# Group 2 of a fused attention and MLP kernel: 16 pairs of W2 rows in seven products behind the output projection, and the softmax maximum in two passes

## The chip, the core and the metric

The kernel runs on one core of one Trainium2 chip. The metric is the device time of one execution in microseconds, as the median of several runs. TensorE does the matmuls and VectorE, ScalarE and GpSimd the rest; SyncE issues most DMAs, and GpSimd those that add into SBUF. In the trace they are PE (PEld: its weight loads), DVE, ACT, POOL and SP.

## The reference

```python
def reference(A_x, A_wqkv, A_wo, B_x, B_w1, B_b1, B_w2, B_b2):
    # B, S, D, F = 1, 2048, 576, 4608; H = 32 heads of 18; window W = 8, dilation 2
    x = A_x
    h = x + _A_ref(_layernorm(x), A_wqkv, A_wo)         # windowed attention
    return h + _B_ref(_layernorm(h), B_w1, B_b1, B_w2, B_b2)

    # _A_ref: qkv = x @ wqkv; each position looks at itself and at the seven
    #         positions 2, 4, ..., 14 before it; softmax over the 8; o @ wo
    # _B_ref: gelu(layernorm(x) @ w1 + b1) @ w2 + b2
```

## The kernel before

The 2048 rows are 16 tiles of 128 rows; row p of tile j is position 16 p + j, so a window of dilation 2 lies in tiles of the same parity. Even tiles keep K and V in `kv_ring[0]` and odd tiles in `kv_ring[1]`; a *halo* load replaces a tile's K or V by the rows shifted by one partition once its last user is done. The tiles are treated in `GROUPS` of two: (14, 12), (10, 8), (6, 4), (2, 0), (15, 13), (11, 9), (7, 5), (3, 1), numbered 0 to 7 by `k`. All instructions stand in the order in which the program issues them on each engine (a manual schedule); nothing reorders them.

One round of the loop over `k` runs these stages for group `k` on TensorE, with the attention of later groups beside them on VectorE:

- **MLP1** (`pm`, line 228): 324 matmuls of 64 rows each; ScalarE's GELU writes `h_all` (line 586). Lists `m1[0]` to `m1[3]` hold what other engines issue ahead of its four visits.
- **Output projection** (`pw`, line 228) for the two tiles c and d of group k + 1: 36 matmuls of 64 rows, from `oT`. `oT` is the attention output turned by DMA: `send_o` stores it to DRAM (`td`, lines 210 and 211) and `read_o` reads it back transposed (line 447).
- **MLP2** (`po`, line 693) for group k: W2's 36 row blocks are 18 pairs. `ROWS[k]` pairs go through seven products (a Strassen-like scheme for 2 x 2 blocks: two tiles by two row blocks, two column halves) and the others through eight plain matmuls (`plain`, steps "11", "12", "21", "22"). All are matmuls of 128 rows. Groups 0 and 1 use plain matmuls throughout (line 605).

The seven products need sums of W2 blocks (`w2_sums`, line 663), made once and kept, and sums of `h_all` blocks (`h_sums`, line 673), made per group. Both are VectorE instructions. `t_slot` and `s_slot` say where the sums lie: in dead parts of `kv_ring`, `x_all` and `q_all`. With pairs beyond `SR` = 12, three H sums of four pairs lie in `q_all` 15, 13 and 11 until `kv_ring[1]` is free.

In `mlp2_fast` the list `steps` is the order on TensorE; a step name calls what `hooks` (the dictionary `x`) holds. "wo" is the output projection; "hc" and "h" are the residual sums with LN2 (`ln2_h`, line 475; `ln2_act`, whose root is the GpSimd power at line 500) and H sums; (n, rows) is product n; "b", "d" and "f" are ScalarE copies of one bank into another (line 782); "6", "7", "in", "exp" and "4" hold LN2's stores and transposing reads (`hnT`, line 516), attention and reloads; "o1" is the output sum of the second tile (line 724).

Attention for the tiles e and f of group k + 2 is, on VectorE: the QK product (`att_qk_a`, line 352) with its additions (361, 370), the softmax maximum and its subtraction (`att_max`, lines 376 and 377), after ScalarE's exponential the sum and division (`att_den`, lines 403 to 405), and in the next round the two PV products (line 409) with additions. `att_qk_a` behind an LN2 is made to wait for the root (`root`).

Before the change, group 2 differs from groups 3 to 6:

```python
ROWS = {2: 12, 3: 16, 4: 16, 5: 16, 6: NM, 7: NM}
steps = [(1, all_), "b", "wo", "hc", "h", "e", (2, all_), ...]          # group 2
steps = ["wo", "hc", (1, all_), "b", "h", "e", (7, lo), (2, all_), ...] # groups 3 to 5
x["7"] += [c_(att_qk_one, f, 1) if k > 2 else c_(att_qk_b, f, 1), c_(att_max, (e, f))]
```

In group 2 the QK product of tile f stands ahead of the H sums (in `m1[3]`), and only its additions stand in "7".

Of the kernel before, what the change touches and what calls it, by code (L numbers as in the profile page):

```python
# [13 lines left out]
F16 = mybir.dt.float16  # L14
# [3 lines left out]
def kernel(  # L18
# [13 lines left out]
    P = 128  # L32
# [23 lines left out]
    GROUPS = [ATT_ORDER[i:i + 2] for i in range(0, NT, 2)]  # L56
# [14 lines left out]
    x_all = wpool.tile([P, NT, D], BF16, name="x_all")  # L71
    q_all = wpool.tile([P, NT, D], BF16, name="q_all")
# [492 lines left out]
    NM = FT // 2  # L565
# [73 lines left out]

    SR = 12  # L640
    ring1_free = [False]
    RING_T = 3 * SR * P

    def s_slot(t, m0, m1):
        if t == 2:
            return h_block(0, 1, m0, m1)
        i = (0, 1, None, 2)[t]
        if m0 < SR:
            return ring_blocks(0, (i * SR + m0) * P, m1 - m0, P)
        if not ring1_free[0]:  # L650
            return q_all[:, 15 - 2 * i, (m0 - SR) * P:(m1 - SR) * P].bitcast(F16).rearrange("p (m c) -> p m c", c=P)
        return ring_blocks(1, 6 * HALF + (i * (NM - SR) + m0 - SR) * P, m1 - m0, P)

    def h_block(odd, i, m0, m1):
# [50 lines left out]
    def c_(fn, *a):  # L705
        return lambda: fn(*a)
# [1 line left out]
    def halves(ap):  # L708
        return ap.rearrange("p (g c) -> p g c", g=2)

    def mlp2_fast(g, rows, tags, wo, hooks, first_wo=False):
        last, summed = wo is None, rows < NM
        q, p, r, s = tags
        j0, j1 = g
        af = psum_pair(q, "po")
        a, f = (af[:, n, 0:HALF] for n in range(2))
        b, d = psum_pair(p, "po")[:, 0, 0:HALF], None
        o0, o1 = (new_o(j, summed) for j in g)
        flat = kv_ring[1][:].rearrange("p w t d -> p (w t d)")
        rest = halves(flat[:, W * 2 * D - 2 * D:W * 2 * D].bitcast(F32))  # L720
        bank = {1: a, 2: a, 3: f, 4: b, 6: b}

        def add(out, x, y):
            nc.vector.tensor_tensor(out=out, in0=x, in1=y, op=ALU.add)

        def last_out():
            nc.vector.tensor_copy(out=o0[:, HALF:HALF + HALF // 2], in_=f[:, 0:HALF // 2])
            nc.scalar.copy(out=o0[:, HALF + HALF // 2:D], in_=f[:, HALF // 2:HALF])
            nc.sync.dma_start(out=out3[:, j0, HALF:D], in_=o0[:, HALF:D])

        def out0(n0, n1):
            if summed:
                nc.scalar.copy(out=halves(o0), in_=af[:, :, 0:HALF])
                return
            add(halves(o0)[:, n0:n1], af[:, n0:n1, 0:HALF], halves(x_of(j0))[:, n0:n1])
            nc.sync.dma_start(out=out3[:, j0, n0 * HALF:n1 * HALF], in_=o0[:, n0 * HALF:n1 * HALF])

        def out1():
            if summed:
                add(o1[:, HALF:D], bank[5], o1[:, 0:HALF])  # L740
                add(o1[:, 0:HALF], b, o1[:, 0:HALF])
                out_sum(j1)
                return
            add(o1[:, 0:HALF], b, rest[:, 0])
            add(o1[:, HALF:D], bank[5], rest[:, 1])
            nc.sync.dma_start(out=out3[:, j1, :], in_=o1)

        def do_rest():
            if summed:
                nc.scalar.copy(out=o1[:, 0:HALF], in_=bank[7])  # L750
                return
            add(rest, bank[7].unsqueeze(1).to_broadcast([P, 2, HALF]), halves(x_of(j1)))

        def take():
            bank[7], bank[5] = (psum_pair(tag, "po")[:, 0, 0:HALF] for tag in (r, s))

        lo, hi, all_ = (0, SR), (SR, rows), (0, rows)
        seed = {"b": (1, 6), "d": (6, 5), "f": (5, 3)}
        does = {
            "wo": lambda: wo((r, s)), "e": take, "rest": do_rest, "o1": out1,  # L760
            "o0": lambda: last_out() if last else out0(0, 2), "lo": lambda: out0(0, 1),
            "11": lambda: plain(0, 0, a, rows), "12": lambda: plain(0, 1, f, rows),
            "21": lambda: plain(1, 0, b, rows), "22": lambda: plain(1, 1, bank[5], rows),
        }
        if rows < NM:
            steps = [(1, all_), "b", "wo", "hc", "h", "e", (2, all_), "11", (6, all_), "d", "6", "7", (7, all_), "rest"] if not first_wo \
                else ["wo", "hc", (1, all_), "b", "h", "e", (7, lo), (2, all_), (6, all_), "6", "d", "rest", "7", "11"] if rows == SR \
                else ["wo", "hc", (1, all_), "b", "h", "e", (7, lo), (2, all_), (6, all_), "6", "7", "d", "11", (7, hi), "rest"]
            steps += ["in", (5, all_), "f", "exp", (4, all_), "21", "22", "o1", "4", (3, all_), "12", "o0", "3"]
        elif not last:  # L770
            steps = ["wo", "hc", (1, all_), "b", "h", "e", (7, lo), (6, all_), "6", "d", "7", (2, all_), (7, hi), "rest", "in",
                     (5, all_), "f", (4, all_), "o1", "4", (3, all_), "o0"]
        else:
            steps = ["e", (1, lo), (7, lo), (1, hi), "b", "h", (7, hi), "rest", (6, all_), "d", (2, all_), "lo",
                     (5, all_), "f", (4, all_), "o1", (3, all_), "o0"]
        for step in steps:
            if isinstance(step, tuple):
                product(step[0], bank[step[0]], *step[1])
            elif step == "f" and last:
                add(f, bank[5], x_of(j0)[:, HALF:D])  # L780
            elif step in seed:
                nc.scalar.copy(out=bank[seed[step][1]], in_=bank[seed[step][0]])
            else:
                call([does[step]] if step in does else hooks.get(step, ()))
# [22 lines left out]
    with tc.manual_schedule(engines={ENG.PE, ENG.Activation, ENG.DVE, ENG.SP, ENG.Pool}):  # L807
# [223 lines left out]
        def wo_visit(*duos, fill=False):  # L1031
            visit([wo_duo(j, tag) for j, tag in duos], (lambda: [ahead[0]() for _ in range(2)]) if fill else None)

        ROWS = {2: 12, 3: 16, 4: 16, 5: 16, 6: NM, 7: NM}
        p, q, r, s = "ABDC"

        gelu_table()
        for k, g in enumerate(GROUPS):
            c, d = GROUPS[k + 1] if k + 1 < len(GROUPS) else (None, None)
            e, f = GROUPS[k + 2] if k + 2 < len(GROUPS) else (None, None)  # L1040
            m1, mid, ia, ib, late_wo = {0: []}, {}, {}, {}, None
# [28 lines left out]
            if k < 2:  # L1070
# [1 line left out]
                mlp2_tile(g, 0, "D", ia)  # L1072
                mlp2_tile(g, 1, "C", ib)
                continue
            rows = ROWS[k]
            x = {n: [] for n in ("hc", "h", "6", "7", "in", "exp", "4", "3")}
            if 2 < k < 7:
                m1[0] += [c_(pv_sum, c), c_(send_o, c), c_(pv_sum, d), c_(read_o, c), c_(send_o, d), c_(read_o, d)]
            if k < 6:
                m1[1] = m1.get(1, []) + [c_(att_qk_one, e, 0)]  # L1080
                m1.setdefault(3, [])
                if k == 2:
                    m1[0] += [c_(pv_sum, d), c_(send_o, d), c_(read_o, d)]
                    m1[3] += [c_(w2_sums, 0, 8, (2, 3)), c_(w2_sums, 8, 12, (2, 3)), c_(w2_sums, 12, 14, (0, 1)), c_(w2_sums, 14, 16, (0, 1)),
                              c_(att_qk_a, f), c_(halo, f, 1)]
                early = {2: (), 5: (0,)}.get(k, (0, 2))
                if k == 3:
                    m1[3] += [c_(w2_sums, 12, 14, (2, 3)), c_(w2_sums, 14, 16, (2, 3))]
                m1[3] += [c_(h_sums, 0, min(rows, SR), early)]
                if k == 5:  # L1090
                    x["h"] += [c_(h_sums, 0, SR, (2,)), c_(h_sums, 0, SR, (1, 3))]
                else:
                    x["h"] += [c_(h_sums, 0, SR, [t for t in range(4) if t not in early])]
                if rows > SR:
                    x["h"] += [c_(h_sums, SR, rows)]
                x["7"] += [c_(att_qk_one, f, 1) if k > 2 else c_(att_qk_b, f, 1), c_(att_max, (e, f))]
                x["exp"] += [c_(exps, e, f)]
                x["4"] += [c_(att_den, e, f)]
            else:
                if k == 6:  # L1100
                    ring1_free[0] = True
                    m1[1].append(c_(w2_sums, 16, NM))
                m1[3] = m1.get(3, []) + [c_(h_sums, 0, SR)]
                if k == 7:
                    mid[3] = {1: [c_(h_sums, SR, 16)]}
                    x["h"] += [c_(h_sums, 16, NM)]
            if k + 3 < len(GROUPS):
                x["in"] += [c_(reload_x, GROUPS[k + 3])]
            wo = None
            if c is not None:  # L1110
                if k == 6:
# [10 lines left out]
                wo = lambda tags: wo_visit((c, tags[0]), (d, tags[1]))  # L1122
# [2 lines left out]
                stores = [c_(out_store, j) for j in GROUPS[k - 1][::-1]]  # L1125
                x["6"] = x["6"] + stores if k == 6 else stores + x["6"]
            mlp1(g, mlp1_plan(p, q, r, s, (r, s, p)), m1, mid)
            if 3 <= k < 7:
                mlp2_fast(g, rows, (s, p, q, r), wo, x, True)
                p, q, r, s = q, r, p, s  # L1130
            else:
                mlp2_fast(g, rows, (q, p, r, s), wo, x)
                p, q, r, s = r, s, p, q


# [28 lines left out]
```

## Time and profile before

| what | us |
|---|---|
| median of 3 runs (lowest to highest) | 360.77 (360.17 to 361.07) |
| the profiled execution | 361.01 |
| its span, first to last instruction | 359.2 |
| TensorE busy in the span | 353.4 |
| VectorE busy | 295.8 |
| ScalarE busy | 235.8 |
| GpSimd busy | 47.3 |

The span is one execution; the time around it (361.01 - 359.2) is start and end. A row of the chain or of a timeline gives its start from the start of the span, its length, the engine, the line of the kernel, what is written and read, and how many instructions are taken together; a bracket gives the engine's idle time before it and what ended that. TensorE's granted clock was 1.000 throughout.

### The profile page before, as it was taken

The numbers are of one execution on the slowest core, as the hardware profiler recorded it, in microseconds if no ns is written. First come the engines' busy times: TensorE is split into PE (matmuls) and PEld (weight loads), VectorE is DVE, ScalarE is ACT, GpSimd is POOL, SyncE is SP. The second block draws the span as 40 slices with busy tenths as digits, with TensorE's granted clock in tenths as the row PEclk, the third lists the DMA queues.
The fourth block names the chain that finished last, engine by engine and source line by source line (L and its number), as shares of the span: only waits on it lengthen the run. The fifth ranks groups of instructions, "written<-read, shape, count | busy, mean of one in ns | idle before, by whom it ended". The sixth has DMA issues, their size and how long they took to land.

```text
span 359.2 us, 11579 instructions
## 1 busy us (share of the span) xinstructions
PE 353.4 (98%) x4953; PEld 289.5 (81%) x4953; DVE 295.8 (82%) x416; ACT 235.8 (66%) x524; POOL 47.3 (13%) x61
## 2 busy tenths in 40 slices
PE   8999999999999999999999999999999999999996
PEld 4777978887788877887788778877887788778874
DVE  5999999999989989998799899989998998520431
ACT  4889757897647783668566956685669566706620
POOL 2241003000212020201200211021102110210000
PEclk9999999999999999999999999999999999999999
DMA  7997799955737584722553545344555253253001
GB/s 242 328 296 168 186 248 294 387 188 137 153 71 123 164 222 84 126 71 49 118 85 82 100 110 84 77 114 108 85 90 102 57 86 56 55 120 51 4 1 34
DMA packets 63492, 46.29 MB, mean 129 GB/s; under 512 B 32192, under 2 KB 61760, under 8 KB 63440
## 3 DMA queue, kind: packets, MB, share of 16 engines
q1 hardware_dynamic: 59472, 41.50, 43.6%
q0 software_dynamic: 3744, 3.84, 9.9%
q8 instruction: 38, 0.62, 0.8%
q10 hardware_dynamic: 224, 0.22, 0.3%
q14 instruction: 14, 0.11, 0.1%
HBM read 23.38 MB, written 12.42 MB: 100 GB/s over the span
## 4 chain that ended last, share of the span: by engine, by line
PE 72%; DVE 20%; DMA 4%; SPq 1%; ACT 1%; issue 1%; DVEq 0%; ACTq 0%
PE pm L228 34%; PE po L693 25%; PE po L605 9%; PE pw L228 4%; DVE prod L361 3%; DVE ln_stats L148 3%; DVE prod L409 3%; DVE prod L352 3%; DVE prod L415 2%; DMA oT<-td 2%; DMA x_all<-in_A_x_dram 1%; ACT h_all L586 1%; SPq L104 1%; DMA td<-q_all 1%; DVE ln_mv L149 1%
## 5 line engine op out<-in xcount | busy, mean ns | idle before, releaser
L228 PE MATMUL pm<-hnT,w_sb 64*128 64x256 bf16 x2304 | 143.0, 269 | 0.0
L586 ACT ACTIVATE h_all<-pm,b_sb 128x256 f16<-128x256 f32 (+1 forms) x288 | 108.4, 495 | 51.2 <-PE pm L228 50.5
L228 PEld LDWEIGHTS <-w_sb 64*128 64x128 bf16 x2304 | 111.7, 94 | 15.1 <-issue 1.7
L693 PEld LDWEIGHTS <-h_all 128*128 128x128 f16 x480 | 46.2, 98 | 13.7 <-issue 1.6
L228 PE MATMUL pq<-wq_sb,xnT 64*128 64x288 bf16 x720 | 54.9, 283 | 0.7 <-DMA wq_sb<-in_A_wqkv_dram 0.2
L228 PEld LDWEIGHTS <-xnT 64*128 64x128 bf16 x864 | 43.4, 94 | 10.9 <-issue 1.4
L361 DVE TENSOR_TENSOR prod<-prod 128x2304 bf16<-128x2304 bf16 (+1 forms) x64 | 44.2, 691 | 2.1
L352 DVE TENSOR_TENSOR prod<-kv_ring,q_all 128x4608 bf16<-128x4608 bf16 x16 | 40.8, 2550 | 2.8 <-POOL ln_rstd L500 2.5
L409 DVE TENSOR_TENSOR prod<-kv_ring,probs 128x4608 bf16<-128x4608 bf16 x16 | 40.9, 2558 | 1.1 <-DMA kv_ring<-kv_dram 0.6
L228 PE MATMUL pm<-hnT,w1h_sb 64*128 64x256 bf16 x288 | 39.2, 269 | 0.0
L693 PE MATMUL po<-w2a_sb,h_all 128*128 128x288 bf16 (+1 forms) x262 | 35.8, 286 | 0.0
L415 DVE TENSOR_TENSOR prod<-prod 128x2304 bf16<-128x2304 bf16 (+1 forms) x32 | 33.9, 1058 | 1.1
L605 PEld LDWEIGHTS <-h_all 128*128 128x128 bf16 x288 | 27.8, 98 | 7.9 <-issue 1.0
L693 PEld LDWEIGHTS <-kv_ring 128*128 128x128 f16 x252 | 24.6, 98 | 6.3 <-DVE kv_ring L673 0.2
L605 PE MATMUL po<-w2a_sb,h_all 128*128 128x288 bf16 x224 | 28.5, 286 | 0.0
L228 PE MATMUL pq<-wqh_sb,xnT 64*128 64x288 bf16 x144 | 27.6, 283 | 0.0
L795 POOL DMA_DIRECT2D x_all<-o_sb x12 | 10.7, 888 | 126.1 <-PE pw L228 73.1
L500 POOL TENSOR_TENSOR ln_rstd<-ln_var,mhalf 128x1 f32<-128x1 f32 x13 | 10.3, 792 | 80.8 <-ACT ln_var L499 80.8
L228 PE MATMUL pw<-wo_sb,oT 64*128 64x288 bf16 x256 | 19.6, 283 | 0.7 <-DMA oT<-td 0.7
L693 PE MATMUL po<-w2b_sb,h_all 128*128 128x288 bf16 (+1 forms) x122 | 19.7, 286 | 0.1
L673 DVE TENSOR_TENSOR kv_ring<-h_all 128x1536 f16<-128x1536 f16 (+3 forms) x9 | 6.8, 760 | 15.8 <-ACT h_all L586 15.8
L161 POOL TENSOR_TENSOR ln_rstd<-ln_veps,mhalf 128x1 f32<-128x1 f32 (+2 forms) x14 | 13.2, 951 | 47.6 <-DVE ln_nmean L489 30.1
(115 smaller groups left out, 401.3 us busy)
## 6 DMA issues: line engine op xcount, KB each, us to landing
w_sb<-in_B_w_dram SPq DMA_DIRECT2D x6, 768.0 KB, 6.1
kv_ring<-kv_dram SPq DMA_DIRECT2D x28, 144.0 KB, 2.3
kv_dram<-kv_ring SPq DMA_DIRECT2D x13, 288.0 KB, 3.7
w2a_sb<-in_B_w_dram SPq DMA_DIRECT2D x3, 1008.0 KB, 10.5
x_all<-in_B_b_dram SPq DMA_DIRECT2D x15, 144.0 KB, 4.1
td<-q_all SPq DMA_DIRECT2D x14, 144.0 KB, 2.0
td<-hn SPq DMA_DIRECT2D x14, 144.0 KB, 1.8
x_all<-h POOLq DMA_DIRECT2D x14, 144.0 KB, 4.6
```

Of the source, the lines that this page charges most:

```text
L148: nc.vector.bn_stats(out=stats[:, i, c, :], in_=src[:, c * HALF:(c + 1) * HALF])
L161: nc.gpsimd.tensor_tensor(out=rstd[:], in0=veps[:], in1=mhalf[:].to_broadcast([P, n]), op=ALU.pow)
L228: last = nc.tensor.matmul(duo["g"][r ^ swap][i], lhsT=lhsT, rhs=rhs, start=(swap == 0 and i == 0 and kt == 0), stop=(swap == 1 and kt == K ...
L352: ins = nc.vector.tensor_tensor(out=prod[:], in0=k_ring[j % 2], in1=q_all[:, j, :].unsqueeze(1) .to_broadcast([P, W, D]), op=ALU.mult).ins
L361: nc.vector.tensor_tensor(out=prod[:, :, o * H:o * H + n], in0=prod[:, :, a * H:a * H + n], in1=prod[:, :, c * H:c * H + n], op=ALU.add)
L409: nc.vector.tensor_tensor(out=prod[:].rearrange("p w (d h) -> p w d h", h=H), in0=v_ring[j % 2].rearrange("p w (d h) -> p w d h", h=H), in ...
L415: nc.vector.tensor_tensor(out=prod[:, 0:n, :], in0=prod[:, 0:n, :], in1=prod[:, n:2 * n, :], op=ALU.add)
L500: ins = nc.gpsimd.tensor_tensor(out=rstd[:], in0=var[:], in1=mhalf[:], op=ALU.pow).ins
L586: pace[0] = nc.scalar.activation(out=hT(grp)[:, f, 0:N], in_=ps[:, r, i * N:(i + 1) * N], func=ACT.Gelu_apprx_tanh, bias=b1_sb[:, f:f + 1] ...
L605: nc.tensor.matmul(banks[half], lhsT=hT(grp)[:, f, i * P:(i + 1) * P], rhs=w2_rows(f)[:, half * HALF:(half + 1) * HALF], start=(f == 0), s ...
L693: nc.tensor.matmul(bank, lhsT=l, rhs=r, start=start, stop=stop, skip_group_check=True)
L795: nc.gpsimd.dma_start(out=x_of(j), in_=o_of.pop(j), accum_op=ALU.add)
```

## The change

- `ROWS` drops to groups 6 and 7; all other fast groups, group 2 among them, use 16 pairs. The steps of group 2 become those of groups 3 to 5: the output projection comes first.
- In group 2 three H sums of the pairs 12 to 15 cannot all lie in `q_all` (tile 13's Q is still wanted), so two of them lie in `x_all` 10 and 8 (`spare`). The reload of x for group 5, which overwrites those, goes behind the last product.
- The W2 sums t = 2 and 3 of the pairs 12 to 15 move from group 3's `m1[3]` to group 2's. Two of the four H sums of group 2 move ahead of the output projection's sums, as in group 3.
- The QK product of tile f in group 2 moves from `m1[3]` to "7". In groups 2 to 5 `att_max` runs over tile e alone ahead of tile f's QK product, and over tile f alone behind it.
- The PSUM tags of group 2 rotate as in groups 3 to 6.

```diff
+    spare = [False]
...
         if not ring1_free[0]:
-            return q_all[:, 15 - 2 * i, (m0 - SR) * P:(m1 - SR) * P].bitcast(F16).rearrange("p (m c) -> p m c", c=P)
+            rows, j = ((q_all, 15), (x_all, 10), (x_all, 8))[i] if spare[0] else (q_all, 15 - 2 * i)
+            return rows[:, j, (m0 - SR) * P:(m1 - SR) * P].bitcast(F16).rearrange("p (m c) -> p m c", c=P)
...
-            steps = [(1, all_), "b", "wo", "hc", "h", "e", (2, all_), "11", (6, all_), "d", "6", "7", (7, all_), "rest"] if not first_wo \
-                else ["wo", "hc", (1, all_), "b", "h", "e", (7, lo), (2, all_), (6, all_), "6", "d", "rest", "7", "11"] if rows == SR \
-                else ["wo", "hc", (1, all_), "b", "h", "e", (7, lo), (2, all_), (6, all_), "6", "7", "d", "11", (7, hi), "rest"]
-            steps += ["in", (5, all_), "f", "exp", (4, all_), "21", "22", "o1", "4", (3, all_), "12", "o0", "3"]
+            steps = ["wo", "hc", (1, all_), "b", "h", "e", (7, lo), (2, all_), (6, all_), "6", "7", "d", "11", (7, hi), "rest", "in",
+                      (5, all_), "f", "exp", (4, all_), "21", "22", "o1", "4", (3, all_), "12", "o0", "3"]
...
-        ROWS = {2: 12, 3: 16, 4: 16, 5: 16, 6: NM, 7: NM}
+        ROWS = {6: NM, 7: NM}
...
-            rows = ROWS[k]
+            rows = ROWS.get(k, 16)
+            spare[0] = k == 2
...
                     m1[3] += [c_(w2_sums, 0, 8, (2, 3)), c_(w2_sums, 8, 12, (2, 3)), c_(w2_sums, 12, 14, (0, 1)), c_(w2_sums, 14, 16, (0, 1)),
-                              c_(att_qk_a, f), c_(halo, f, 1)]
-                early = {2: (), 5: (0,)}.get(k, (0, 2))
-                if k == 3:
-                    m1[3] += [c_(w2_sums, 12, 14, (2, 3)), c_(w2_sums, 14, 16, (2, 3))]
+                              c_(w2_sums, 12, 14, (2, 3)), c_(w2_sums, 14, 16, (2, 3))]
+                early = (0,) if k == 5 else (0, 2)
...
-                x["7"] += [c_(att_qk_one, f, 1) if k > 2 else c_(att_qk_b, f, 1), c_(att_max, (e, f))]
+                x["7"] += [c_(att_max, [e]), c_(att_qk_one, f, 1), c_(att_max, [f])]
...
-                x["in"] += [c_(reload_x, GROUPS[k + 3])]
+                x["3" if k == 2 else "in"] += [c_(reload_x, GROUPS[k + 3])]
...
-            if 3 <= k < 7:
-                mlp2_fast(g, rows, (s, p, q, r), wo, x, True)
+            if k < 7:
+                mlp2_fast(g, rows, (s, p, q, r), wo, x)
                 p, q, r, s = q, r, p, s
             else:
                 mlp2_fast(g, rows, (q, p, r, s), wo, x)
-                p, q, r, s = r, s, p, q
```

More of the change, by code (lines that the diff above doesn't have):

```diff
@@ L709, in halves, with mlp2_fast @@
         return ap.rearrange("p (g c) -> p g c", g=2)
-    def mlp2_fast(g, rows, tags, wo, hooks, first_wo=False):
+    def mlp2_fast(g, rows, tags, wo, hooks):
         last, summed = wo is None, rows < NM
@@ L1093 @@
                     x["h"] += [c_(h_sums, 0, SR, [t for t in range(4) if t not in early])]
-                if rows > SR:
-                    x["h"] += [c_(h_sums, SR, rows)]
-                x["7"] += [c_(att_qk_one, f, 1) if k > 2 else c_(att_qk_b, f, 1), c_(att_max, (e, f))]
+                x["h"] += [c_(h_sums, SR, rows)]
+                x["7"] += [c_(att_max, [e]), c_(att_qk_one, f, 1), c_(att_max, [f])]
                 x["exp"] += [c_(exps, e, f)]
```

## The prediction

> **What bounds the kernel now.** I read the page first, for the engine that the end hangs on.
>
> ```profile
> PE 353.4 (98%) x4953; PEld 289.5 (81%) x4953; DVE 295.8 (82%) x416; ACT 235.8 (66%) x524; POOL 47.3 (13%) x61
> PE 72%; DVE 20%; DMA 4%; SPq 1%; ACT 1%; issue 1%; DVEq 0%; ACTq 0%
> ```
>
> TensorE is busy for 98% of the span. The chain's 20% on VectorE and its DMA share could still lie in the stage that the change edits, so I read the chain of waits in order of time (start, length, what), from group 2's MLP2 to group 6's. Here pm is MLP1, pw the output projection, po MLP2.
>
> ```profile
> 160.17 1.58 PE po L693 x12
> 161.75 2.31 PE pw L228 x36
> 164.06 14.82 PE po L693 x120
> 178.88 17.79 PE pm L228 x324
> 196.68 2.21 PE pw L228 x36
> 198.88 15.84 PE po L693 x128
> 214.72 15.83 PE pm L228 x289
> 230.56 2.81 DMA oT<-td
> 233.41 1.77 PE pw L228 x26
> 235.18 15.79 PE po L693 x128
> 250.97 17.79 PE pm L228 x324
> 268.76 2.21 PE pw L228 x36
> 286.75 17.79 PE pm L228 x324
> 304.55 2.32 PE pw L228 x36
> ```
>
> From 160 us on VectorE is not on the chain: matmuls stand end to end, with one DMA between them. So here a microsecond is won by fewer matmuls or by taking away a stall of TensorE, and nothing that VectorE saves counts for itself.
>
> The rows show two stalls. Group 4 takes 235.18 - 214.72 = 20.46 us from the start of MLP1 to its first MLP2 matmul, group 3 takes 198.88 - 178.88 = 20.00: 0.46 us are lost to the DMA row, the transposing read of the second tile's attention output (oT), without which the second half of pw cannot begin. Group 6's pw takes 2.32 instead of 2.21: 0.11, the same read.
>
> **Part 1: group 2's products.** Before, twelve pairs of W2 rows go through seven products (84 matmuls) and six pairs take 8 plain ones each (48): 132, as the rows have it (12 + 120). After, 16 pairs take 112 and two take 16: 128. One matmul is 15.79 / 128 = 0.1234 us, so four are 0.49. The order also matters. The 12 products ahead of pw take 1.58, where 12 x 0.1234 is 1.48, and that pw takes 2.31 instead of 2.21: each time TensorE goes from 64-row to 128-row matmuls or back, 0.10 us are lost. Group 2 goes pm, po, pw, po: three such changes. Groups 3 to 5 go pm, pw, po: one. Group 2 takes their order, and so loses two changes, 0.20. Together that is 0.69. The whole block gives the same: 1.58 + 2.31 + 14.82 = 18.71 against group 3's 2.21 + 15.84 = 18.05, that is 0.66. I take 0.66, since group 2 now gets group 3's VectorE order too, and with it group 3's 0.05 (15.84 instead of 15.79).
>
> **Part 2: what pw now waits for, 1.58 us earlier.** These are rows of SyncE's queue, with the landing times of the oT reads and of the output stores below.
>
> ```profile
> 151.84 1.20 SPq L447 DMA_TRANSPOSE oT<-td  x1
> 153.71 1.97 SPq L798 DMA_DIRECT2D out_dram<-x_all  x2
> 181.87 0.33 SPq L347 DMA_DIRECT2D kv_ring<-kv_dram  x1
> 226.60 0.34 SPq L210 DMA_DIRECT2D td<-q_all  x1
> DMA to landing us min/median/max: 2.6/3.0/4.5
> DMA to landing us min/median/max: 3.1/3.6/5.2
> ```
>
> Group 2's last oT read is issued at 151.84; even at the slowest landing, 4.5, it is there by 156.4, before 160.17. This costs nothing. Two of the new H sums of four pairs go to rows 10 and 8 of x_all, which the output stores issued from 153.71 must have left: by 155.7 + 5.2 = 160.9, and VectorE gets there near 162.72 + 1.41 + 2 x 0.95 = 166.0 (part 3). Nothing again. The reload of x (two DMAs) now waits until the last product has read those rows, so until shortly before group 3's MLP1 (178.88 - 0.66 = 178.2). Behind it on SyncE stands the V halo load at 181.87, which waits for a VectorE product anyway, and the reloaded rows are first added in group 4. The K halo load of the second tile goes, with the product that it waits for (159.45 + 2.55 = 162.0), to a place behind the LN2 stores and ahead of the transposing reads for the next MLP1. Groups 3 and 4 already have that order on SyncE, and their next MLP1 starts at 214.72 and 250.97 with no DMA before it in the chain. If that cover were gone, MLP1 would wait by as much as the read lands late.
>
> **Part 3: VectorE in group 2.** Rows of VectorE's timeline.
>
> ```profile
> 159.45 2.55 DVE L352 TENSOR_TENSOR prod<-kv_ring,q_all 128x4608 bf16<-128x4608 bf16 x1
> 176.91 1.03 DVE L403 TENSOR_REDUCE den<-logits 128x64 f32<-128x512 f32 x1
> 195.91 0.39 DVE L663 TENSOR_TENSOR kv_ring<-w2a_sb,q_all 128x576 f16<-128x576 bf16 x1
> 197.32 0.95 DVE L673 TENSOR_TENSOR kv_ring<-h_all 128x1536 f16<-128x1536 f16 x1
> 199.18 1.41 DVE L475 TENSOR_TENSOR h<-pw,x_all 128x576 f32<-128x576 f32 x2
> 204.92 2.56 DVE L352 TENSOR_TENSOR prod<-kv_ring,q_all 128x4608 bf16<-128x4608 bf16 x1 [1.01 <-POOL ln_rstd L500]
> 211.08 1.03 DVE L376 TENSOR_REDUCE peak<-logits 128x64 f32<-128x512 f32 x1
> 212.14 0.69 DVE L377 TENSOR_TENSOR logits<-logits,peak 128x512 f32<-128x512 f32 x1
> 212.75 0.94 DVE L724 TENSOR_TENSOR o_sb<-po,o_sb 128x288 f32<-128x288 f32 x2
> 213.61 1.04 DVE L403 TENSOR_REDUCE den<-logits 128x64 f32<-128x512 f32 x1
> 248.61 0.95 DVE L724 TENSOR_TENSOR o_sb<-po,o_sb 128x288 f32<-128x288 f32 x2
> 249.48 1.02 DVE L403 TENSOR_REDUCE den<-logits 128x64 f32<-128x512 f32 x1
> 276.57 2.56 DVE L352 TENSOR_TENSOR prod<-kv_ring,q_all 128x4608 bf16<-128x4608 bf16 x1 [0.44 <-POOL ln_rstd L500]
> 285.42 1.02 DVE L403 TENSOR_REDUCE den<-logits 128x64 f32<-128x512 f32 x1
> ```
>
> The QK product at 159.45 leaves this place. The four W2 sums of group 3 (195.91 to 197.32, 1.41) and two H sums (197.32 to 199.18, 1.86) come in. VectorE then reaches the LN2 sums (L475) at 159.45 + 1.41 + 1.86 = 162.72, some 0.3 to 0.4 behind the end of pw at 160.17 + 2.21 = 162.38. Group 3 shows the same lateness, 199.18 against 198.88, and pays 0.05 for it, which is counted. Group 3 without those four sums becomes like group 4, whose block has 15.79: 0.05 won.
>
> **Part 4: the split maximum, groups 2 to 5.** One pass over both tiles takes 1.03 + 0.69 = 1.72 us. A pass over one tile is seen earlier in the trace:
>
> ```profile
> 99.94 0.59 DVE L376 TENSOR_REDUCE peak<-logits 128x32 f32<-128x256 f32 x1
> 100.56 0.42 DVE L377 TENSOR_TENSOR logits<-logits,peak 128x256 f32<-128x256 f32 x1
> ```
>
> Two of them take 2.02, so a group's VectorE work grows by 0.30. But the first pass now stands where VectorE waited 1.01 for GpSimd's LN2 root before the QK product (204.92), and it lasts 1.01. In groups 2 to 4 the product does not move. In group 5 the wait is only 0.44, and the product moves by 0.57. Behind the product 1.72 shrinks to 1.01: 0.71 won in groups 2 to 4, 0.14 in group 5.
>
> [...]
>
> What it wins can only reach TensorE through oT: VectorE starts the softmax sum (L403), then both PV products, their stores and transposing reads, and the second half of pw waits for the last. Against the MLP1 start of the group that waits, the sum starts at 176.91 - 178.88 = -1.97 (group 3, no stall), -1.11 (group 4, 0.46), -1.49 (group 5, none), -1.33 (group 6, 0.11). So stalls begin when it starts later than some 1.45 before MLP1. It cannot go earlier than about -1.49: ahead of it stands the output sum L724, which needs products 4 and the plain ones, and behind those only 20 matmuls (2.47 us) remain. At 248.61 L724 stands 2.36 ahead of MLP1, and that is this floor, while at 212.75 it stands only 1.97 ahead, because VectorE was late. After the change group 2's softmax sum stands at the floor (its spare 0.48 goes, since only 20 instead of 24 matmuls follow), group 3's too: it loses 1.41 of W2 sums and 0.71 of the maximum, and needs only 0.38 of that. So group 4's stall, 0.46, goes or leaves 0.08. Group 5's sum moves from -1.33 to the neighbourhood of -1.45, and group 6's 0.11 becomes 0.02: 0.09 won.
>
> **The sum.** 0.66 + 0.05 + 0.46 + 0.09 = 1.26 us. The profiled execution took 361.01 (span 359.2), 0.24 over the median of three, 360.77. On its own time that is 359.75, on the median 359.51. I forecast 359.5. About 0.3%, or 1.08 us, is what a measurement of this kernel can tell from no change: the bounds are 359.69 and 361.85.
>
> **Rivals.**
> *The stalls stay.* Group 4's store and read took 230.56 - 226.60 = 3.96 until the transposing read was issued, and 2.81 more. If the DMA engines and not VectorE make that late, only 0.66 + 0.05 are won: 360.06. For it: 3.96 is long for one tile. Against it: the four starts and stalls above fall in order.
> *VectorE sets the pace.* If the root is ready before the first maximum begins, there is no wait to hide in, and each of four groups pays its 0.30 on a VectorE that TensorE then follows: 360.77 - 0.66 + 1.20 = 361.31, no measurable change. Against it: the 1.01 us wait, and no VectorE row on the chain after 160. [...]
> *The oT reads come late in three groups.* All of groups 3 to 5 now live at the floor, with no spare. If a store takes group 4's 3.96 and its read the slowest landing seen, 4.5, that is 8.46 in place of group 4's 6.77, and pw stalls for 0.08 + 1.69 = 1.77. In one group this gives 360.77 - 0.71 + 1.77 = 361.83, in all three 365.4. The point from which it decides is 6.8 us from store to landing. Both ends are in the trace, but not together in one of these groups; the median landing is 3.0.
>
> **How the numbers follow.** The forecast has 0.66: its centre lies 0.18 under the bound of 359.69, and the three runs lie within 0.6 below and 0.3 above their median, so I count 0.53 of it as faster and 0.13 as within. The stalls that stay get 0.20, of which 0.02 faster, as the median may hold more such stalls than the profile. VectorE's pace gets 0.04, within. The late reads get 0.10, slower; one group brings it to the bound, at 361.83, and a second one past it. Faster 0.55, same 0.35 (0.13 + 0.18 + 0.04), slower 0.10. The range goes from 359.0 (the forecast and half a microsecond of spread) to 360.6 (the first rival and the same): outside are the late reads and some of VectorE's case.
>
> **What would show it.** Right: group 2's block from MLP1's end to the next MLP1 takes about 18.05; no DMA row on the chain in any pw from group 2 on; the QK product of the second tile follows the first maximum with no idle time in groups 2 to 4; the softmax sum starts about 1.49 before MLP1 in groups 3, 4 and 5. Wrong: a DMA row ahead of pw, idle time of VectorE that ends on the stores of rows 10 and 8, or an MLP1 that waits for hnT.

## The result, and the profile after

| | before | after |
|---|---|---|
| median, us | 360.77 (360.17 to 361.15, 7 runs) | 359.67 (359.12 to 360.21, 7 runs) |
| ratio after / before | | 0.9969, 95% interval 0.9957 to 0.9981 |
| the profiled execution, us | 361.01 | 359.39 |
| its span, us | 359.2 | 357.6 |

Faster by 1.10 us, 0.31%. The forecast was 359.5 with a range of 359.0 to 360.6. Helper lines move by two: L693 is now L695, L663 L665, L673 L675, L724 L726.

The page of after, busy time and the chain's shares by engine:

```profile
PE 351.8 (98%) x4949; PEld 289.1 (81%) x4949; DVE 298.5 (83%) x428; ACT 236.0 (66%) x524; POOL 47.5 (13%) x61
PE 72%; DVE 20%; DMA 3%; SPq 1%; ACT 1%; issue 1%; DVEq 0%; ACTq 0%
```

Four matmuls fewer, 12 VectorE instructions and 2.7 us of VectorE more, and the span is shorter: VectorE still does not set the time in these stages. The chain of waits of after, in order of time from group 2's MLP1 (start, length, what):

```profile
142.09 17.79 PE pm L228 x324
159.88 2.21 PE pw L228 x36
162.09 15.80 PE po L695 x128
177.88 17.79 PE pm L228 x324
195.68 2.21 PE pw L228 x36
197.88 15.79 PE po L695 x128
213.67 17.79 PE pm L228 x324
231.46 2.21 PE pw L228 x36
233.66 15.79 PE po L695 x128
...
285.24 17.79 PE pm L228 x324
303.03 2.21 PE pw L228 x36
```

There is one pattern now, pm, pw, po, in every group, and no DMA row. Read against the rows of before:

| step | before | after | won | forecast |
|---|---|---|---|---|
| group 2, end of MLP1 to next MLP1 | 18.71 | 2.21 + 15.80 = 18.01 | 0.70 | 0.66 |
| group 3, its po | 15.84 | 15.79 | 0.05 | 0.05 |
| group 4, MLP1 to first po matmul | 20.46 | 233.66 - 213.67 = 19.99 | 0.47 | 0.46 |
| group 6, its pw | 2.32 | 2.21 | 0.11 | 0.09 |

The four make 1.33 of the 1.62 by which the profiled executions differ. The other 0.29 lies ahead of the change: group 2's MLP1 starts at 142.09 instead of 160.17 - 17.79 = 142.38. Over all profiles of this study that start lies between 141.36 and 142.70, for kernels whose work up to there is the same or nearly so. A block between two rows of the chain is therefore a finer measure than a span or a median.

VectorE's timeline of after, in groups 2, 3, 4 and 5 (the bracket is idle time and what ended it):

```profile
166.99 0.58 DVE L376 TENSOR_REDUCE peak<-logits 128x32 f32<-128x256 f32 x1
167.61 0.43 DVE L377 TENSOR_TENSOR logits<-logits,peak 128x256 f32<-128x256 f32 x1
168.09 2.56 DVE L352 TENSOR_TENSOR prod<-kv_ring,q_all 128x4608 bf16<-128x4608 bf16 x1
...
175.53 0.95 DVE L726 TENSOR_TENSOR o_sb<-po,o_sb 128x288 f32<-128x288 f32 x2 [0.27 <-PE po L695]
176.40 1.04 DVE L403 TENSOR_REDUCE den<-logits 128x64 f32<-128x512 f32 x1
...
203.59 2.56 DVE L352 TENSOR_TENSOR prod<-kv_ring,q_all 128x4608 bf16<-128x4608 bf16 x1 [0.44 <-POOL ln_rstd L500]
...
212.18 1.04 DVE L403 TENSOR_REDUCE den<-logits 128x64 f32<-128x512 f32 x1
...
239.38 2.56 DVE L352 TENSOR_TENSOR prod<-kv_ring,q_all 128x4608 bf16<-128x4608 bf16 x1 [0.44 <-POOL ln_rstd L500]
...
283.75 1.02 DVE L403 TENSOR_REDUCE den<-logits 128x64 f32<-128x512 f32 x1
```

The softmax sum (L403) starts 177.88 - 176.40 = 1.48 before MLP1 in group 2, and 1.49 before it in groups 3, 4 (249.45 - 247.96) and 5. L726 ahead of it waits for TensorE (0.27 in group 2): that is the floor which the prediction had worked out. Of groups 2 to 4, the QK product follows the first maximum with no idle time in group 2 alone; in groups 3 and 4 it still waits 0.44 for the root in this profile.

### The profile page after: what moved, and what is told of

The parts are those of the page before. It is cut to its first block, busy times and chain, and to the rows that moved or that the text cites. A ratio compares the mean times of both kernels' runs of the same rounds, so it can differ in the third digit from the quotient of the medians.

```text
span 357.6 us, 11589 instructions
## 1 busy us (share of the span) xinstructions
PE 351.8 (98%) x4949; PEld 289.1 (81%) x4949; DVE 298.5 (83%) x428; ACT 236.0 (66%) x524; POOL 47.5 (13%) x61
## 4 chain that ended last, share of the span: by engine, by line
PE 72%; DVE 20%; DMA 3%; SPq 1%; ACT 1%; issue 1%; DVEq 0%; ACTq 0%
PE pm L228 34%; PE po L695 25%; PE po L605 9%; PE pw L228 4%; DVE prod L361 3%; DVE ln_stats L148 3%; DVE prod L409 3%; DVE prod L352 3%; DVE prod L415 2%; DMA x_all<-in_A_x_dram 1%; ACT h_all L586 1%; SPq L104 1%; DVE ln_mv L149 1%; DMA td<-q_all 1%; DMA oT<-td 1%
## 5 line engine op out<-in xcount | busy, mean ns | idle before, releaser
L695 PEld LDWEIGHTS <-h_all 128*128 128x128 f16 x464 | 44.7, 98 | 13.1 <-issue 1.4
L695 PE MATMUL po<-w2a_sb,h_all 128*128 128x288 bf16 (+1 forms) x252 | 34.1, 286 | 0.0
L695 PEld LDWEIGHTS <-kv_ring 128*128 128x128 f16 x252 | 24.7, 98 | 6.2
L675 DVE TENSOR_TENSOR kv_ring<-h_all 128x1536 f16<-128x1536 f16 (+3 forms) x9 | 6.8, 753 | 16.2 <-ACT h_all L586 16.2
L695 PE MATMUL po<-w2b_sb,h_all 128*128 128x288 bf16 (+1 forms) x112 | 18.8, 286 | 0.1
```

The costliest lines, as they stand in the source:

```text
L695: nc.tensor.matmul(bank, lhsT=l, rhs=r, start=start, stop=stop, skip_group_check=True)
```

## The experiments

The theory of the prediction: group 4's stall depends on when the softmax sum starts, with a threshold near 1.45 before MLP1. The rival: the DMAs decide it, and the start of the sum is only one of the things that move them. Each ratio below is to runs of the kernel before in the same series; their medians are 360.38 in the first series (the first four experiments), 360.33 in the second (the two delays) and 360.49 in the third (the last four).

**Twelve pairs instead of 16** takes the first part of the change out and keeps the order and the split maximum.

```diff
-        ROWS = {6: NM, 7: NM}
+        ROWS = {2: SR, 6: NM, 7: NM}
...
-                              c_(w2_sums, 12, 14, (2, 3)), c_(w2_sums, 14, 16, (2, 3))]
+                if k == 3:
+                    m1[3] += [c_(w2_sums, 12, 14, (2, 3)), c_(w2_sums, 14, 16, (2, 3))]
...
-                x["h"] += [c_(h_sums, SR, rows)]
+                if rows > SR:
+                    x["h"] += [c_(h_sums, SR, rows)]
```

> The changed kernel with one part undone: group 2 runs 12 pairs in seven products again (132 matmuls), in the new order, and the W2 sums of pairs 12 to 15 go back to group 3. Theory (matmul count, two mode changes, stalls set by when VectorE starts the softmax sum): group 2's block is 18.01 + 4 x 0.1234 = 18.50 us, and no DMA row stands on the chain in any pw, because the split maximum alone wins more than the 0.38 that group 3 lacked. Median about 360.15. Rival (the stall of group 4 goes only because the W2 sums left group 3): the DMA row is back in group 4's pw with some 0.4, median about 360.5.

360.07 (359.53 to 361.17), ratio to before 0.9992 (0.9978 to 1.0007). Its chain, groups 2 and 3:

```profile
160.20 2.21 PE pw L228 x36
162.41 16.28 PE po L695 x132
...
209.57 4.96 DMA hnT<-td
...
214.57 17.86 PE pm L228 x324
```

Group 2's block is 2.21 + 16.28 = 18.49: 0.22 less than before by the order alone, 0.48 more than after for four matmuls. Both halves of the prediction's 0.66 are the size it gave, measured against the first profile of after. No oT read is on the chain, although the four W2 sums are back in group 3. The DMA row is another read, hnT for MLP1, which held the next MLP1 up by about 0.17 (198.68 + 15.79 = 214.47 for its start, where 198.68 is the first po matmul, and 17.79 for its length). The prediction had named that wait as a sign of being wrong; it turned up here, not in the changed kernel.

**The old order with 16 pairs** puts twelve pairs of product 1 ahead of the output projection in group 2 again.

```diff
-            steps = ["wo", "hc", (1, all_), "b", "h", "e", ...
+            steps = [*(["wo", "hc", (1, all_)] if g != GROUPS[2] else [(1, lo), "wo", "hc", (1, hi)]), "b", "h", "e", ...
...
-            if k < 7:
+            if k == 2:
+                mlp2_fast(g, rows, (q, p, r, s), wo, x)
+                p, q, r, s = r, s, p, q
+            elif k < 7:
```

> The changed kernel with group 2's first product cut in two: 12 of its pairs stand ahead of the output projection, as before, with the old PSUM tags. The matmul count is that of the changed kernel (128). Theory: the two changes between 64-row and 128-row matmuls come back, group 2's block is 18.01 + 0.20 = 18.21, everything else stays; median about 359.85. Rival (the order cost nothing and the whole 0.70 came from matmuls or from a wait that the new order removed): the block stays at 18.01, or grows by more than 0.3.

360.29 (359.79 to 360.67), ratio 0.9992 (0.998 to 1.0004). Group 2's block is 178.61 - 159.61 = 19.00, 0.99 over after. The theory had 18.21; the rival's second branch, a wait that the new order removes, had a growth of over 0.3, and that is what the rows show. The two changes between 64-row and 128-row matmuls cost 92 and 95 ns in the gaps between the matmuls' starts, as forecast. The other 0.8 is in these rows of TensorE's and ScalarE's timelines:

```profile
163.84 0.68 ACT L497 ACTIVATE hn<-h 128x576 bf16<-128x576 f32 x1 [1.46 <-DVE h L475]
165.76 0.39 ACT L783 COPY po<-po 128x288 f32<-128x288 f32 x1
166.20 1.88 PE L695 MATMUL po<-w2a_sb,h_all 128*128 128x288 bf16 x14 [0.63 <-ACT po L783]
```

Product 2 waits for ScalarE's copy "b" of product 1. The copy stands behind LN2's first activations on ScalarE, and those wait for the residual sum on VectorE. With all 16 pairs of product 1 behind pw, TensorE has 28 matmuls there ahead of product 2 (16 of product 1, 12 of product 7), 3.5 us; with four pairs it has 16, 2.0 us. So "the output projection comes first" wins more than these two changes once 16 pairs are used: against this profile of after it is worth 0.99, not 0.20. The prediction had not seen this cover.

**The split maximum alone**, in the kernel before.

```diff
-                x["7"] += [c_(att_qk_one, f, 1) if k > 2 else c_(att_qk_b, f, 1), c_(att_max, (e, f))]
+                x["7"] += [c_(att_max, [e]), c_(att_qk_one, f, 1) if k > 2 else c_(att_qk_b, f, 1), c_(att_max, [f])]
```

> The kernel before with the split maximum alone: in groups 2 to 5 the first tile's maximum stands ahead of the second tile's products (in group 2 ahead of their additions), nothing else is changed. Theory: group 2's block stays 18.71; the softmax sum of group 3 starts at the floor of -1.49 instead of -1.11, so the 0.46 stall in group 4's pw goes, and group 6's 0.11 nearly goes; in all about 0.5 less than before in the profile, median about 360.3. Rival 1 (the DMA engines set the stall): the DMA row stays in group 4's pw, median 360.8. Rival 2 (VectorE sets the pace, and each split costs 0.30): slower by up to 1.2, median 361.3 to 362.

360.12 (359.75 to 360.72), ratio 0.9991 (0.9978 to 1.0004). Group 2's block stays at 18.71; the pw of groups 4 and 6 take 2.21 and 2.20, with no DMA row, as the theory had it. Two rows of its chain:

```profile
214.25 17.79 PE pm L228 x324
232.04 2.21 PE pw L228 x36
```

**The joint maximum in the changed kernel** is the opposite.

```diff
-                x["7"] += [c_(att_max, [e]), c_(att_qk_one, f, 1), c_(att_max, [f])]
+                x["7"] += [c_(att_qk_one, f, 1), c_(att_max, (e, f))]
```

> The changed kernel with the split undone: one maximum over both tiles behind the second tile's products in groups 2 to 5. Theory: group 2 now carries the work that group 3 carried before, so its softmax sum starts about 1.1 before MLP1, and the 0.46 stall stands in group 3's pw instead of group 4's; group 4's stays away (group 3 is as light as group 4 was); group 6's 0.11 is back. About 0.57 more than the changed kernel, median about 360.2. Rival (the DMA engines set the stall): no DMA row in group 3's pw, median as the changed kernel, 359.7.

359.36 (358.49 to 360.33), ratio 0.9967 (0.9953 to 0.9982). The expected stall in group 3 is not there, and group 6's 0.11 is not back (its pw takes 2.21). VectorE's timeline and the chain:

```profile
176.62 1.03 DVE L403 TENSOR_REDUCE den<-logits 128x64 f32<-128x512 f32 x1
...
177.78 17.79 PE pm L228 x324
195.57 2.20 PE pw L228 x36
```

The sum starts 1.16 before MLP1 and pw takes 2.20. In the kernel before, 1.11 went with a stall of 0.46. Five hundredths can hardly make that on a threshold of 1.45: the first crack in the theory.

**Two doses of delay** put one more VectorE sum (its result is overwritten) ahead of the softmax sum in groups 2 to 5 of the changed kernel: over 8 heads (0.29 us from its start to the next one's) or over 32 (0.54 to 0.63). The edit is shown for 8 heads; for 32, both 8s are 32.

```diff
+    def delay(e):
+        nc.vector.tensor_reduce(out=den[:, sides([e]), 0:8], in_=logit_of([e])[:, :, :, 0:8].rearrange("p i w h -> p i h w"), axis=AX.X, op=ALU.add)
...
-                x["4"] += [c_(att_den, e, f)]
+                x["4"] += [c_(delay, e), c_(att_den, e, f)]
```

> The changed kernel with VectorE held up ahead of the softmax sum in groups 2 to 5: one more sum over the positions, for 8 heads of the first tile (64 elements), written where the full sum overwrites it. Estimated at 0.26 from the maximum's 0.59 for 256 and 1.03 for 512 elements. Theory (the second half of pw waits for a chain that starts with the softmax sum, stalls begin near -1.45 before MLP1): the sum starts near -1.22, and groups 3 to 6 each stall by 0.2 to 0.35, together 0.8 to 1.4 us over the changed kernel. Rival (there is spare beyond the floor, the DMA engines decide): no stall in most groups, less than 0.3 in all.

> The same with the first tile's whole sum (256 elements), 0.62 us of VectorE ahead of the softmax sum in groups 2 to 5. Theory: the sum starts near -0.87, and groups 3 to 6 each stall by 0.5 to 0.75, about 0.24 more than at -1.11 before; together 2.0 to 3.0 us over the changed kernel. Rival (the DMA engines decide): stalls under 0.3 per group.

8 heads: 359.41 (358.76 to 360.06), ratio 0.9974 (0.9962 to 0.9985). Only group 4 stalls, as the chain and VectorE's timeline have it:

```profile
212.29 1.05 DVE L403 TENSOR_REDUCE den<-logits 128x64 f32<-128x512 f32 x1
...
213.49 15.57 PE pm L228 x283
229.06 2.85 DMA oT<-td
...
231.96 1.77 PE pw L228 x26
```

The sum starts 1.20 before MLP1, earlier than in group 3 of the joint maximum (1.16), and yet 213.49 + 20.00 = 233.49 becomes 233.73 (the first po matmul): 0.24 lost there and nothing elsewhere. 32 heads: 360.47 (359.07 to 361.49), ratio 1.0003 (0.9987 to 1.0019), with 0.20, 0.27 and 0.10 lost to oT in groups 3, 4 and 6, none in group 5, and 0.28 to ScalarE's copy in group 3. Both lost much less than start for start, and not in all groups: 0.24 where the theory had 0.8 to 1.4 in all, and 0.85 where it had 2.0 to 3.0.

**Second profiles of both kernels.**

> The kernel before, unchanged, in a second profiled execution. Theory: group 4's pw stalls by 0.3 to 0.5 again and group 6's by about 0.1, since VectorE's starts are the same in every execution; MLP2 of group 2 takes 18.71 again. Rival (the DMA engines set the stall): the stalls stand elsewhere or are gone.

> The changed kernel, unchanged, in a second profiled execution. Theory: group 2's block 18.01, no DMA row in a pw from group 2 on, or one of at most 0.1, as the reads land close to the time when they are needed. Rival (the late reads): a stall of over 0.5 in one group, seen in some executions only.

Before: 360.24, group 4's stall 0.21 and none in group 6, with the same instructions as in the first profile. In group 4's pw, the ten matmuls ahead of the wait take 0.61 with it, where 2.21 - 1.77 = 0.44 is their time without:

```profile
232.09 0.61 PE pw L228 x10
...
232.75 1.77 PE pw L228 x26
```

After: 359.6, no DMA row, and 0.17 lost in group 2 (its block takes 18.18) at 165.7, where product 2 waits for the copy "b". So the size of the stall is not a constant of the kernel. The two profiles of before lose 0.57 and 0.21 in groups 4 and 6 together.

**What moves the read.** By SyncE's rows, group 4's store (L210) to transposing read (L447) takes 230.56 - 226.60 = 3.96 before, and in after:

```profile
225.17 0.34 SPq L210 DMA_DIRECT2D td<-q_all  x1
227.15 1.76 SPq L447 DMA_TRANSPOSE oT<-td  x1
```

1.98. The chain got 2 us shorter at this point, although the sum started only 0.38 earlier. The DMA view shows a difference, for 226.9 to 228.9 of before (KB of one, us to landing):

```profile
q8 instruction: 1, 0.02, 4.4%
td<-q_all SPq DMA_DIRECT2D x1, 16.0 KB, 3.5
```

and for 225.4 to 227.2 of after, where no such queue is listed:

```profile
td<-q_all SPq DMA_DIRECT2D x1, 16.0 KB, 1.5
```

One packet of an instruction queue lies among the store's rows, and the store's last 16 KB land 2 us later. The page of after has the whole queue:

```profile
q8 instruction: 38, 0.62, 0.7%
```

0.62 MB in 38 packets are 16 KB each. PE and PEld issue 2 x 4949 = 9898 instructions, 260 for each packet, and in the trace's list of packets one starts after every 253 or so of them on average (152 to 352 from one packet to the next in the first profiles of both kernels): I read it as TensorE's instruction stream. TensorE itself shows no cost of it here: group 4's round, MLP1 to MLP1, takes 249.45 - 213.67 = 35.78 in after, and 35.78 and 35.79 in two more profiles of that kernel, with such packets in it. Whether a DMA beside such a packet is held up is what the next runs ask.

If this is right, the stall can be moved with no touch to VectorE: fewer or more TensorE instructions early in the kernel shift all later packets against the stores, 36 of them by some 1.0 us (my estimate: MLP1's 648 instructions take 17.79). Fewer of them in the kernel before should then take the packet off group 4's store, and the stall with it.

**Fewer TensorE instructions at the start** of the kernel before, and **more of them** in the changed kernel. The warm-up matmuls' results are used nowhere.

```diff
# fewer, in before
-        for n in [512] * 8 + [P] * 8:
+        for n in [512] * 10:
...
-        for n in range(12):
+        for n in range(0):
# more, in after
-        for n in [512] * 8 + [P] * 8:
+        for n in [512] * 2 + [P] * 32:
```

> The kernel before with 18 fewer warm-up matmuls on TensorE at the start (16 become 10, 12 become none), that is 36 fewer TensorE instructions with their weight loads; their output is used by nothing. Every later instruction keeps its order, and VectorE's work is untouched, so group 4's softmax sum starts where it did, about 1.05 before MLP1. [...] Rival (the start of the sum alone): the store takes 3.7 to 4.0 again, and group 4 stalls by 0.2 to 0.45 as in the two profiles of the kernel before. The median falls by the stall at most, 0.2 to 0.5, too little to carry a verdict; the rows of group 4 carry it.

> The changed kernel with 18 more warm-up matmuls at the start (six of 512 columns give way to 24 of 128), 36 more TensorE instructions; nothing uses their output. Theory (instruction fetch): the packet that came just behind group 4's store in the changed kernel now comes some 1.0 us earlier, on top of it: SyncE issues group 4's second oT read 3.4 to 3.9 after the store instead of 2.0, although the softmax sum still starts 1.49 before MLP1. The read then lands about 11.55 + 3.75 + 2.85 = 18.15 after MLP1's start, 0.16 ahead of the 18.31 at which pw needs it, so the stall is 0 to 0.1 if the landing is the usual one. Rival (the start of the sum alone): the read is issued 2.0 after the store as in the changed kernel. The time is that of the changed kernel within its scatter, by either.

Fewer, group 4, in VectorE's timeline, SyncE's and the chain:

```profile
213.75 1.04 DVE L403 TENSOR_REDUCE den<-logits 128x64 f32<-128x512 f32 x1
226.74 0.34 SPq L210 DMA_DIRECT2D td<-q_all  x1
228.81 2.05 SPq L447 DMA_TRANSPOSE oT<-td  x1
...
214.86 17.79 PE pm L228 x324
232.65 2.20 PE pw L228 x36
...
250.64 13.60 PE pm L228 x247
264.24 5.15 DMA oT<-td
```

The sum starts 1.11 before MLP1, exactly as in the kernel before, and the read now follows the store by 2.07 instead of 3.96: group 4 has no stall. So the start of the sum alone does not make the stall: with the packet out of the store's way, the same start has none. But the median did not fall: 360.9 (360.21 to 361.72), ratio 1.0007 (0.9992 to 1.0021). Group 5, which had never stalled, has a read that takes 5.15 to land, and loses 271.20 - 250.64 - 20.00 = 0.56 to it (271.20 is the first po matmul). In the list of packets one starts 4.07 after that store's last issue, during the read, where before it started at 2.86.

More, group 4, in SyncE's timeline and in the DMA view for 224.8 to 226.8:

```profile
224.46 0.34 SPq L210 DMA_DIRECT2D td<-q_all  x1
228.24 1.21 SPq L447 DMA_TRANSPOSE oT<-td  x1
```

```profile
q8 instruction: 1, 0.02, 4.2%
td<-q_all SPq DMA_DIRECT2D x1, 16.0 KB, 3.3
```

3.78 instead of 1.98, with the packet among the store's rows, as the theory had it, and still no stall: the read lands 18.03 after MLP1's first matmul (212.88), 0.28 before the second half of pw starts. Here the sum starts 1.49 before MLP1; the packet alone does not make the stall either. 359.17 (358.65 to 359.44), ratio 0.9958 (0.9942 to 0.9975).

These two runs also show whose the packets are. In all 14 profiles of this study the packet at group 4's store starts when PE and PEld have started 6571 to 6595 instructions. Its time moves with that count: it starts 1.89 after the store's last issue with 36 instructions fewer, where it was 1.03 in before, and 0.46 after it with 36 more, where it was 1.98 in after.

**The changed kernel and the joint maximum in one series.**

> The changed kernel itself, timed beside its twin with the joint maximum. 359.4 to 359.9, and 0.7 to 1.4 less than the kernel before. All theories expect this.

> The changed kernel with the joint maximum of both tiles in groups 2 to 5, again, in the same series as the changed kernel. If the split maximum is worth something in itself (the prediction gave it group 4's stall, together with the earlier output sum), this is 0.2 to 0.5 slower than the changed kernel. If the room that the other parts of the change make suffices, the two are equal within 0.3, and group 4 has no DMA row in pw here either.

359.48 (358.94 to 360.61), ratio 0.9975 (0.9963 to 0.9987), and 359.26 (359.07 to 360.09), ratio 0.9968 (0.9956 to 0.998). Split or joint, the time is the same within what can be told, and neither has a DMA row in group 4's pw. This third profile of the changed kernel does lose time elsewhere, as its chain shows for groups 2 and 6:

```profile
162.70 3.54 PE po L695 x28
166.26 12.41 PE po L695 x100
...
303.81 2.30 PE pw L228 x36
```

Group 2's block takes 178.67 - 160.50 = 18.17 (the starts of the next MLP1 and of pw), since product 2 again waits for the copy "b", as in the second profile. Group 6's pw takes 2.30: the late oT read that the kernel before had there is back once, with the softmax sum 1.49 before MLP1.

Nor is the kernel with more warm-up matmuls told apart from these two. No version beats the changed kernel measurably.

## Why the prediction was right, and which of its steps were not

- **Group 2's block, 0.66 forecast, 0.70 measured in the first profile.** Twelve pairs gave 18.49: 0.22 come from the order and 0.48 from the four matmuls. The prediction's 0.20 and 0.49 hold. The block lies 0.04 under the forecast since group 3's own 0.05 appears in it as only 0.01. What the prediction put at nothing is product 2's wait for the copy "b": it takes 0.17 and 0.16 back in the second and third profile of the changed kernel, which keep 0.53 and 0.54. Each change between 64-row and 128-row matmuls costs 0.09 to 0.10 us; the trace does not show what that time is spent on.
- **Group 4's stall, 0.46 forecast, 0.47 measured, by a step that was half right.** "Stalls begin when it starts later than some 1.45 before MLP1" does not hold by itself. In group 4 the profiles have:

  | profile | sum ahead of MLP1 | packet behind the store's last issue | lost |
  |---|---|---|---|
  | before, first | 1.11 | 1.03 | 0.46 |
  | before, second | 1.09 | 1.08 | 0.21 |
  | delay of 8 heads | 1.20 | 1.16 | 0.24 |
  | delay of 32 heads | 0.86 | 0.77 | 0.27 |
  | fewer instructions | 1.11 | 1.89 | 0 |
  | more instructions | 1.49 | 0.46 | 0 |
  | after, first | 1.49 | 1.98 | 0 |

  So group 4 stalled where a late sum and a packet at the store came together, and with one of them alone it did not (one profile with the late sum, one with the packet). It is a sum of times and no strict rule: in group 3 of the second run with the joint maximum the sum starts 1.17 ahead with a packet 0.04 behind the store's last issue, and the read still lands 0.19 before the second half of pw starts. In 14 profiles, its read was issued 3.24 to 3.57 after the store's last issue (L211, 0.4 behind L210) where the packet started 0.46 to 1.16 after that issue (five profiles), and 1.60 to 1.68 where it started 1.33 or more after it (nine). The earlier sum helps in two ways: it gives 0.38 of margin, and it can bring the store out of the packet's way (with the split maximum alone the packet starts 1.34 behind the store's last issue instead of 1.03). After had both. The direction of the prediction's step was right; what it missed is the 2 us that the packet puts into the path. So there is no threshold in the start of the sum alone, and the size of 0.46 is that of one profile; the forecast's sum took it whole, though the step itself let 0.08 stay. That the four starts and stalls "fall in order", the argument against the first rival, rested on four points of one profile, of which group 6's is a matter of the packet (below).
- **The first rival, "the stalls stay", named the right part and the wrong outcome.** The prediction noted that "3.96 is long for one tile". That was the packet. The stalls went because the store time is not fixed, and because the earlier sum leaves room for it.
- **The floor, 1.49 before MLP1: right** in groups 2 to 5 (1.48, then 1.49 three times).
- **The split maximum: it hid as forecast, and won nothing that the runs can tell.** In the twin with the joint maximum, VectorE waits 1.08 for the root in group 3, and the first maximum fills that. In two profiles of the changed kernel the root itself took 0.83 and 0.84 instead of 0.55 in groups 3 and 4, which leaves 0.44 of idle time, so "no idle time in groups 2 to 4" fails there; in the third profile it took 0.55 and there is none. Why it took longer is open. This costs nothing, as VectorE is not the bound, and the joint maximum has the same time. VectorE setting the pace (361.31) did not happen; its 2.7 us of added work stay off the chain.
- **The late reads did not happen, but were near.** In group 3 of the changed kernel the store takes 3.74, with a packet at it, and the read lands 0.25 before the second half of pw starts in the first profile, 0.12 in the second.
- **Group 6, 0.09 forecast, 0.11 measured, by luck.** Before, its read took 4.36 to land, with a packet starting 2.33 after the read's issue, and in after 2.78, with one starting 2.49 after it. The second profile of before has no stall with the sum at the same 1.33, and the third profile of the changed kernel has one of 0.09 with the sum at 1.49. So this is chance, not the sum's start.
- **The sum.** 1.26 was forecast for one profiled execution and 1.33 found in its blocks; the medians differ by 1.10, and by 360.49 - 359.48 = 1.01 in the third series. Over three profiles of the changed kernel and two of before, group 2 wins 0.59 on average, group 3 has its 0.05, the stalls of before are worth 0.39, and group 6's one stall in after costs 0.03: 1.00. So part of the 1.33 is luck: the profile of before had the larger stalls, and the first profile of after none. This is worked out from five profiles only.

## What to carry to other kernels

Group 4's stall, which ended on a DMA, was a sum of issue, landing and a packet beside the store (3.96 from store to read with it in before, 1.98 in after); before a shorter chain of instructions alone is credited with removing such a stall, compare issue and landing in two profiles of the same kernel. Fixed work (matmuls fewer, changes between 64-row and 128-row ones) was priced from rows to a few hundredths here (0.49 and 0.20 forecast, 0.48 and 0.22 measured), while a stall with a margin of some tenths could only have been given as a range (0.46 and 0.21 in two profiles of one kernel). When matmuls move from one side of a stage to the other, look at what they cover there: the matmuls behind the projection hide a ScalarE copy (0.39 long), and even in the changed kernel their 3.54 were too short for it in two of three profiles (0.17 and 0.16 lost).

## What the runs showed of the hardware

A 16 KB packet of an instruction queue came after 253 TensorE instructions on average in before and 252 in after, and took 0.9 to 1.9 us in the DMA engines there. Where one started 0.46 to 1.16 us after the last issue of group 4's store, the store's last 16 KB landed in 3.2 to 3.5 us instead of 1.5 or 1.6. TensorE itself shows no wait for such a packet in the rounds of group 4 that are given above, but through the DMA beside it TensorE lost up to 0.56 us. Adding 36 TensorE instructions at the start moved such a packet onto group 4's store 220 us later, and removing 36 moved it off that store and lost time to a read in group 5, with the same instructions in the same order there. The transposing read landed late beside such packets too: in the 14 profiles, from group 2 on, 35 of 36 oT reads without a packet in their time landed in 2.65 to 3.0 us (the other in 3.46), and 41 of 42 in which one started 0.7 to 2.35 us after the issue took 3.3 to 4.7 (the other 2.93). No run was made for this alone. That the store's last rows wait behind the packet on one DMA engine is argued from the times; the trace does not name the engine. That the packets belong to TensorE is inferred from nearly the same running count of TensorE's instructions at group 4's packet in all 14 profiles (6571 to 6595) and from the two runs that moved it.
